# A retention layer and a feed-forward layer on one core: the last turned layer's weight operands get places of their own, and the order tables are written anew

## The chip, the core and the metric

One core of a Trainium2 chip runs the whole kernel. The engines' names are those of the profile: PE (TensorE matmuls) and PEld (its weight loads), DVE (VectorE), ACT (ScalarE), POOL (GpSimd) and SP (SyncE, which here only issues DMAs). SBUF is the core's on-chip memory, PSUM the memory that PE writes. The metric is the device time of one execution in microseconds (us); less is better.

## The reference

```python
gamma = 1.0 - 2.0 ** (-5.0 - np.arange(H)); scale = 1.0 / np.sqrt(D)
for t in range(S):                                  # B, H, S, D = 4, 8, 768, 64
    state = gamma * state + np.einsum('bhd,bhe->bhde', k[:, :, t], v[:, :, t])
    y[:, :, t] = scale * np.einsum('bhd,bhde->bhe', q[:, :, t], state)
x = y.transpose(0, 2, 1, 3).reshape(B * S, H * D)   # 3072 tokens of 512
h = x @ w_in                                        # 512 -> 2048
sp = np.maximum(h, 0.0) + np.log1p(np.exp(-np.abs(h)))
return (h * erf(sp)) @ w_out                        # 2048 -> 512
```

All arrays are float32.

## The kernel before, in words

The retention is computed in chunks of the sequence: within a chunk by masked scores, and across chunks by a carried state. For each chunk q, k and v are loaded, scaled (L795 and L804 on DVE, products of two SBUF tiles; the latter on ACT, L800, in some chunks) and transposed (L813). The results are the rows of x, 256 tokens at a time.

The feed-forward layer takes its first 512 tokens by plain matmuls: `hidden` (L1121) and `project` (L1161). A few of these projections are left over and placed among the later work (`('proj', tile, from, to)` in the tables). The other 2560 tokens use a fast multiplication: 26 products of sums take the place of the plain block products. The sums of the weights (30 of them, `W_SUMS`) are made once, for `w_in` at L614 on DVE or POOL, and for `w_out` at L1477 on POOL or by ACT and an accumulating DMA (L1482, L1487). The `w_out` operands are then stored to a DRAM tile `w_out_d` (`spill`, L1452). The sums of the activations (`X_ORDER`) are made on DVE.

The 2560 tokens are five macros of 512. A macro is four first layers, `first_layer(g)`, and one turned layer, `second_layer(M)`:

- A first layer makes h for a group, 26 products of two matmuls of 128 columns (L1260). Each product's result in PSUM is read into the SBUF tile `arena`: added by DVE (L1274), or, on the first touch of a part, copied by DVE (L1277, L1279; those that `F_DVE` names) or by ACT (L1281, L1283). The very first group is plain (`PLAIN`). After it come softplus and erf on ACT (L1307), and four halves of the gate h·erf, each 1024 columns or two times 512, on DVE or POOL (L1316).
- A turned layer is 26 products of four matmuls of 256 columns (L1391), in the profile eight matmul records each. They hold the `w_out` operand as stationary weights and stream the gated block or a sum of gated blocks. Block sums (L1378, `add`) run on POOL, and in the last macro on DVE. Products are read from four PSUM banks into the result tile `R` (L1399, L1403 and L1405 on DVE, L1401 on ACT). A finished part is transposed by DVE (L1438) and goes out in four DMAs of 32 KB (L1441), by `put`.

The stationary operand of each product is loaded from `w_out_d` into one of four slots of a ring, `WS` (`load_operand`, L1334, 256 KB each). `refill`, ahead of each product, keeps four operands loaded beyond those used. The queue of each load is a letter of `LOAD_FIRST`, `LOAD_LATER` or `LOAD_LAST` (y is SP, s ACT, g POOL); `LOAD_LAST` is 12 times SP and then 14 times ACT.

The order of all this is written out in tables. Every engine and every DMA queue works in the order in which the program issues. For each kind of first layer (0 to 3 in the first macro, a to d in the middle ones, w to z in the last) a row of `AT` has two lists. The first says what is issued behind which of the 26 products: `prod` is one turned product of the macro before, `chunk` one step of the next chunk's preparation, `gate`, `erf`, `op` a sum of w_out, `in` and `in0` sums of w_in, `kick` a wait of POOL for DVE (a DVE copy of one column, L1343, which a POOL copy reads, L1344). The second says what comes behind them all. Further tables give the order of the products (`F_ORDER`; `FIRST_STEPS`, `S_STEPS` and `LAST_STEPS` for the turned layers), which W_in sums are POOL's (`W_IN_POOL`), and what stands ahead of the first first layer (`PRE`).

The turned layer of a macro starts while the first layers of the next one run (`prod`), so that its products fill PE between first-layer products. The last macro has no successor: behind its last first layer come two gates of 1024 columns on DVE, the rest of the turned layer before it, and then all but the first three products of its own turned layer:

```python
    for half in range(2):
        gate(NG - 1, half)
    while active:
        product()
```

`w_in_sb`, the SBUF tile with the 26 operands of W_in, has two halves (`s`) used by first layers in turn; nothing reads a half again behind its last first layer.

Of the kernel before, what the change touches and what calls it, by code (L numbers as in the profile page):

```python
# [23 lines left out]
P = 128  # L24
# [12 lines left out]
N_W, N_X = 26, 18  # L37
# [98 lines left out]
X_ORDER = (1, 0, 2, 6, 5, 12, 13, 9, 4, 7, 14, 8, 15, 3, 17, 10, 16, 11)  # L136
# [4 lines left out]
W_ORDERED = (0, 1, 2, 4, 16, 3, 5, 6, 10, 7, 20, 15, 24, 8, 13, 9, 17, 11, 23, 28, 26, 25, 12, 18, 21, 14, 22, 29, 19, 27)  # L141
# [4 lines left out]
AT = {0: ([(1, 'prod'), (1, 'chunk'), (2, 'spill'), (2, 'spill'), (3, 'in', 19), (6, 'in', 16), (6, 'op'), (8, 'in0', 4),  # L146
      (8, 'in', 3), (8, 'prod'), (9, 'in', 2), (9, 'put', 0), (9, 'prod'), (9, 'in0', 8), (11, 'op'), (12, 'op'),
      (12, 'proj', 1, 0, 2), (12, 'in0', 14), (13, 'in', 25), (13, 'in', 26), (13, 'spill'), (13, 'in', 7),
      (14, 'kick'), (14, 'kick'), (15, 'chunk'), (16, 'chunk'), (16, 'in', 6), (16, 'spill'), (16, 'idle'),
# [5 lines left out]
     [('rest',), ('softplus',), ('proj', 2, 2, 4), ('xs', 3), ('begun',), ('xs', 4), ('prod',), ('prod',),  # L155
      ('proj', 2, 1, 2), ('xs', 1), ('proj', 3, 1, 2), ('in', 30), ('xs', 3), ('prod',), ('prod',), ('xs', 13)]),
 1: ([(1, 'in0', 27), (1, 'proj', 1, 2, 4), (2, 'kick'), (2, 'op'), (3, 'in0', 30), (4, 'prod'), (5, 'kick'), (5, 'op'),
      (5, 'chunk'), (5, 'op'), (7, 'prod'), (8, 'op'), (9, 'chunk'), (10, 'erf', 1), (10, 'gate', 0, 0, 'g'),
      (13, 'prod'), (16, 'chunk'), (17, 'gate', 0, 1, 'v'), (18, 'kick'), (18, 'idle'), (20, 'in', 3), (21, 'put', 2),
      (22, 'chunk'), (24, 'put', 1), (24, 'gate', 1, 0, 'g'), (24, 'gate', 1, 1, 'v'), (26, 'op')],  # L160
     [('rest',), ('xs', 2), ('xs', 4), ('softplus',), ('prod',), ('prod',), ('begun',), ('xs', 15), ('prod',),
      ('proj', 3, 3, 4), ('prod',), ('xs', 1), ('xs', 2)]),
 2: ([(1, 'op'), (1, 'chunk'), (1, 'prod'), (1, 'put', 3), (2, 'kick'), (6, 'op'), (10, 'erf', 1),
      (11, 'gate', 0, 0, 'g'), (11, 'prod'), (13, 'gate', 1, 1, 'g'), (13, 'gate', 1, 0, 'g'), (13, 'gate', 0, 1, 'g'),
      (14, 'op'), (15, 'chunk'), (17, 'op'), (17, 'op'), (18, 'prod'), (20, 'op'), (20, 'chunk'), (20, 'chunk'),
      (21, 'op'), (23, 'refill'), (25, 'op'), (25, 'idle')],
     [('rest',), ('prod',), ('xs', 1), ('xs', 14), ('prod',), ('softplus',), ('xs', 5), ('prod',), ('xs', 2),
      ('begun',), ('prod',), ('xs', 2)]),
# [15 lines left out]
 'c': ([(1, 'chunk'), (1, 'gate', 1, None, 'v'), (5, 'chunk'), (5, 'chunk'), (8, 'next'), (13, 'chunk'), (13, 'prod'),
        (15, 'prod'), (17, 'chunk'), (20, 'gate', 0, 1, 'v'), (21, 'idle'), (24, 'chunk'), (25, 'gate', 0, 0, 'v'),
        (26, 'chunk'), (26, 'kick'), (26, 'prod')],
       [('rest',), ('xs', 3), ('refill',), ('begun',), ('softplus',), ('erf', 0), ('prod',), ('prod',), ('xs', 2),
        ('xs', 5), ('xs', 8), ('prod',), ('prod',), ('xs', 6)]),
 'd': ([(1, 'chunk'), (2, 'kick'), (3, 'chunk'), (6, 'gate', 1, None, 'g'), (7, 'gate', 0, None, 'g'), (10, 'new'),
        (10, 'chunk'), (12, 'chunk'), (14, 'prod'), (17, 'chunk'), (18, 'chunk'), (24, 'chunk'), (26, 'idle')],  # L190
       [('rest',), ('softplus',), ('refill',), ('xs', 7), ('erf', 0), ('begun',), ('prod',), ('append',), ('prod',),
        ('xs', 8), ('prod',), ('xs', 3), ('prod',), ('xs', 1)]),
 'w': ([(1, 'chunk'), (2, 'gate', 1, None, 'v'), (2, 'gate', 0, None, 'v'), (3, 'prod'), (6, 'chunk'), (6, 'kick'),
        (7, 'next'), (10, 'idle'), (12, 'chunk'), (12, 'chunk'), (13, 'prod'), (14, 'chunk'), (19, 'chunk'),
        (22, 'chunk'), (25, 'prod')],
# [4 lines left out]
        (23, 'prod'), (24, 'chunk'), (26, 'chunk')],  # L200
# [3 lines left out]
        (6, 'next'), (8, 'prod'), (11, 'chunk'), (11, 'chunk'), (12, 'chunk'), (13, 'prod'), (16, 'chunk'),  # L204
        (19, 'chunk'), (21, 'idle'), (26, 'prod'), (26, 'chunk')],
       [('rest',), ('softplus',), ('refill',), ('prod',), ('begun',), ('erf', 0), ('xs', 5), ('prod',), ('xs', 6),
        ('xs', 3), ('xs', 8), ('prod',), ('prod',), ('xs', 2)]),
 'z': ([(1, 'chunk'), (1, 'gate', 0, None, 'g'), (3, 'gate', 1, 1, 'v'), (4, 'kick'), (4, 'prod'),
        (5, 'gate', 1, 0, 'v'), (5, 'chunk'), (6, 'kick'), (7, 'chunk'), (10, 'idle'), (14, 'chunk'), (15, 'kick'),
        (15, 'kick'), (15, 'chunk'), (20, 'new'), (20, 'chunk'), (26, 'chunk')],  # L210
       [('rest',), ('refill',), ('softplus',), ('xs', 5), ('erf', 0), ('prod',), ('prod',), ('begun',), ('xs', 4),
# [35 lines left out]
BEGUN = {0: 'smMb',  # L247
 1: 'smMb',
 2: 'smMb',
 3: 'smMb',  # L250
 'a': 'smbM',
 'b': 'smbM',
 'c': 'sMmb',
 'd': 'sMmb',
 'w': 'smbM',
 'x': 'smbM',
 'y': 'sMbm',
# [1536 lines left out]
```

## Time and profile before

| | |
|---|---|
| median of 3 runs | 668.21 us (664.67 to 668.76) |
| profiled execution, its own time | 662.88 us |
| its span (first to last instruction) | 660.8 us |
| mean granted PE clock | 0.996 |
| PE busy | 645.8 us, 6112 matmuls |
| DVE, ACT, POOL busy | 483.8, 309.9, 298.0 us |
| block sums on POOL (L1378) | 75 of 2361 ns |
| turned matmuls (L1391) | 1040, 235.9 us busy |
| operand loads (L1334) on ACT, on SP | 102, 20 |

The profile is of one execution. Its own time is lower than the three timed runs, which are of the same program; sums of durations from it belong to 662.88. "Busy" counts the time in which an engine executes, so 98% for PE means that 15 us of the span are left without a matmul. A granted clock under 1 means that matmuls ran slower in a part of the time; that time counts as busy. The stages that are told apart below: first the plain part and the sums, to 155 us; the first macro's first layers, to 210; the repeated part of first layers with turned products between them, to 593; the last first layer's end, to 607.4; the last turned layer, to 656.2; the last outputs.

### The profile page before, as it was taken

Reading aid. Unit: us, or ns where it says so; the run is one execution under the profiler, and the core shown is the slowest. Engines: PE = TensorE matmul, PEld = TensorE weight load, DVE = VectorE, ACT = ScalarE, POOL = GpSimd, SP = SyncE. Lnnn points to the kernel's source line nnn. Section 1 sums busy time; section 2 is a strip of 40 time slices with the busy share of each in tenths; the row PEclk is TensorE's granted clock in tenths of the full one; section 3 lists DMA queues with packets and bytes.
Section 4 is the critical chain, followed back from the end, with each engine's and each line's share of the span. In section 5 each row is a group of like instructions: output and inputs, shape, how many; then the busy total and the mean of one; then the engine's idle time right before and its main releaser. Section 6 shows DMA issues by size and latency. Waiting matters only on the chain.

```text
span 660.8 us, 16104 instructions
## 1 busy us (share of the span) xinstructions
PE 645.8 (98%) x6112; PEld 544.0 (82%) x6112; DVE 483.8 (73%) x1148; ACT 309.9 (47%) x527; POOL 298.0 (45%) x251
## 2 busy tenths in 40 slices
PE   8999999998899999999999999999999999999897
PEld 7744444476798999999989999999999999999786
DVE  5999889995888846767856857856856944856683
ACT  3468594433574654455453455463554542533200
POOL 1000063767457687316565337475237368344000
PEclk9999999999999999999999999999999999999999
DMA  9999886776557455464564564554554521342565
GB/s 188 231 261 237 173 245 110 135 192 142 146 135 211 109 135 124 106 144 97 132 137 95 139 135 100 134 139 94 128 123 105 127 81 48 110 95 58 155 172 116
DMA packets 221597, 91.55 MB, mean 139 GB/s; under 512 B 185808, under 2 KB 200272, under 8 KB 221520
## 3 DMA queue, kind: packets, MB, share of 16 engines
q1 hardware_dynamic: 198720, 51.50, 38.0%
q10 hardware_dynamic: 17888, 27.08, 14.4%
q0 software_dynamic: 4912, 11.94, 6.6%
q8 instruction: 48, 0.79, 0.5%
q14 instruction: 29, 0.24, 0.1%
HBM read 74.47 MB, written 13.11 MB: 133 GB/s over the span
## 4 chain that ended last, share of the span: by engine, by line
PE 91%; DVE 3%; DMA 2%; SPq 1%; issue 1%; ACT 0%; POOL 0%; DVEq 0%; ACTq 0%; POOLq 0%
PE o L1391 33%; PE hp L1260 18%; PE r L1260 14%; PE hp L1121 8%; PE o L1161 7%; PE r L1037 1%; PE hp L893 1%; PE r L1047 1%; PE hp L990 1%; DVE arena L1274 1%; SPq L373 1%; PE r L1235 1%; DMA kq<-in_k_dram 1%; PE o L750 1%; PE r L779 1%
## 5 line engine op out<-in xcount | busy, mean ns | idle before, releaser
L1391 PE MATMUL o<-arena 128*128 128x256 f32 x1040 | 235.9, 381 | 1.7 <-DMA arena<-w_out_d 1.7
L1391 PEld LDWEIGHTS o<-arena 128*128 128x128 f32 x1040 | 193.0, 190 | 27.1 <-DVE arena L1399 2.1
L1378 POOL TENSOR_TENSOR arena<-arena 128x1024 f32<-128x1024 f32 x75 | 175.8, 2361 | 20.0 <-PE o L1391 15.7
L1260 PE MATMUL hp<-xs,w_in_sb 128*128 128x128 f32 x812 | 118.8, 278 | 2.1 <-DVE arena L1274 2.0
L1260 PEld LDWEIGHTS hp<-xs,w_in_sb 128*128 128x128 f32 x812 | 106.0, 193 | 4.8 <-DVE arena L1274 2.1
L1274 DVE TENSOR_TENSOR arena<-arena,hp 128x256 f32<-128x256 f32 x184 | 75.1, 417 | 25.6 <-PE hp L1260 17.2
L1260 PE MATMUL r<-xs,w_in_sb 128*128 128x128 f32 x632 | 92.4, 277 | 0.5 <-ACT arena L1281 0.2
L1344 POOL COPY idle_out<-turn 128x1 f32<-128x1 f32 x45 | 13.0, 289 | 157.4 <-DVE turn L1343 157.4
L1260 PEld LDWEIGHTS r<-xs,w_in_sb 128*128 128x128 f32 x632 | 81.9, 193 | 2.2 <-issue 0.8
L1399 DVE TENSOR_TENSOR arena<-arena,o 128x256 f32<-128x256 f32 x90 | 37.1, 417 | 63.4 <-PE o L1391 61.4
L1274 DVE TENSOR_TENSOR arena<-arena,r 128x256 f32<-128x256 f32 x158 | 62.8, 416 | 17.6 <-PE r L1260 13.6
L1121 PE MATMUL hp<-xT,w_in_sb 128*128 128x512 f32 (+2 forms) x144 | 56.5, 548 | 0.0
L1260 PE MATMUL hp<-xT,w_in_sb 128*128 128x128 f32 x296 | 45.7, 277 | 3.5 <-DVE arena L1279 1.8
L1121 PEld LDWEIGHTS hp<-xT,w_in_sb 128*128 128x128 f32 x144 | 25.8, 190 | 27.0 <-issue 24.6
L1260 PEld LDWEIGHTS hp<-xT,w_in_sb 128*128 128x128 f32 x296 | 39.8, 192 | 5.7 <-issue 2.6
L1281 ACT COPY arena<-r 128x256 f32<-128x256 f32 x53 | 19.7, 373 | 51.6 <-PE r L1260 21.4
L1056 ACT COPY xT<-r 128x256 f32<-128x256 f32 x33 | 10.8, 375 | 63.0 <-PE r L1047 63.0
L1316 POOL TENSOR_TENSOR arena<-arena,e_even 128x1024 f32<-128x1024 f32 (+1 forms) x19 | 36.3, 1926 | 8.5 <-ACT e_even L1307 8.5
L1307 ACT ACTIVATE e_even<-e_even 128x2048 f32<-128x2048 f32 x20 | 38.2, 1912 | 0.2
L1401 ACT ACTIVATE arena<-o 128x256 f32<-128x256 f32 x25 | 9.3, 378 | 58.8 <-PE o L1391 58.8
L1260 PE MATMUL r<-xT,w_in_sb 128*128 128x128 f32 x236 | 36.2, 276 | 0.3 <-DVE arena L1274 0.2
L722 POOL COPY idle_out<-arena 128x1 f32<-128x1 f32 x1 | 0.6, 592 | 78.9 <-ACT arena L1139 78.9
(185 smaller groups left out, 972.5 us busy)
## 6 DMA issues: line engine op xcount, KB each, us to landing
arena<-w_out_d ACTq DMA_DIRECT2D x102, 256.0 KB, 2.8
arena<-in_moe_w_out_dram SPq DMA_DIRECT2D x12, 512.0 KB, 6.1
kq<-in_k_dram SPq DMA_DIRECT2D x23, 256.0 KB, 4.3
v<-in_v_dram SPq DMA_DIRECT2D x23, 256.0 KB, 3.4
arena<-w_out_d SPq DMA_DIRECT2D x20, 256.0 KB, 3.0
out_dram<-arena SPq DMA_DIRECT2D x154, 32.0 KB, 2.5
kq<-in_q_dram SPq DMA_DIRECT2D x284, 16.0 KB, 2.3
kb<-in_k_dram SPq DMA_DIRECT2D x276, 16.0 KB, 2.4
```

The lines of the kernel that those rows point to most:

```text
L1056: nc.scalar.copy(x[r], pp[r][:, :2, :])
L1121: nc.tensor.matmul(HP_[ft][:, t], w_in_of(ft, kk), XC[0][:, kk, t], start=(kk == 0), stop=(kk == n_k - 1),)
L1161: nc.tensor.matmul(O[0][tt].rearrange("p (c x) -> p c x", c=4), E[g][:, u * TCH + tt * P : u * TCH + (tt + 1) * P], w_out_of(ft), start=(f ...
L1260: nc.tensor.matmul(to[:, u, :], w_in_sb[:, s, w, u * P : (u + 1) * P], x_at(x), start=first and u == 0, stop=True, skip_group_check=True,)
L1274: nc.vector.tensor_tensor(h, h, of, op=ALU.add if plus else ALU.subtract)
L1281: nc.scalar.copy(h, of)
L1307: nc.scalar.activation(e_even[:, at], e_even[:, at], AF.Erf)
L1316: engine.tensor_tensor(x, x, e_even[:, half * BL : (half + 1) * BL][:, at], op=ALU.mult)
L1344: nc.gpsimd.tensor_copy(idle_out, turn)
L1378: engine.tensor_tensor(block(blocks[to]), *ins, op=OP[sign])
L1391: nc.tensor.matmul(to, WS[:, used % 4, u], rhs[:, u * 2 * P : (u + 1) * 2 * P], start=first and u == 0, stop=True, skip_group_check=True,)
L1399: nc.vector.tensor_tensor(r, r, to, op=ALU.add if plus else ALU.subtract)
```

## The change

The last turned layer's 26 operands no longer pass through the ring. `tail_operand(k)` is a place in `w_in_sb`: operands 0 to 12 lie in the half that the next-to-last first layer read, 13 to 25 in that of the last one. `load_tail` issues one load on the queue that `TAIL` names, SP for all. Thirteen are issued behind odd products of the last first layer, and then one behind each product of the last turned layer. `refill` and `load_operand` stop ahead of them, and `LOAD_LAST` is gone.

```diff
     def load_operand():
-        if loaded < len(W_ORDER):
+        if loaded < len(W_ORDER) - N_W:
...
+    def tail_operand(k):
+
+        s, at = (NG - 2 - G0 + k // 13) % 2, k % 13 * 2
+        return w_in_sb[:, s, at : at + 2].rearrange("p a (u c) -> p (a u) c", c=P)
+
+    def load_tail():
+
+        nonlocal tail_loaded
+        k = tail_loaded
+        ENGINES[TAIL[k]].dma_start(
+            tail_operand(k).rearrange("p u c -> p (u c)"), w_out_d[W_ORDER[len(W_ORDER) - N_W + k]]
+        )
+        tail_loaded += 1
...
         def multiply(n, at):
+            in_tail = used - (len(W_ORDER) - N_W)
+            operand = WS[:, used % 4] if in_tail < 0 else tail_operand(in_tail)
             for u in range(FG):
                 nc.tensor.matmul(
-                    to, WS[:, used % 4, u], rhs[:, u * 2 * P : (u + 1) * 2 * P],
+                    to, operand[:, u], rhs[:, u * 2 * P : (u + 1) * 2 * P],
...
             used += 1
+            if in_tail >= 0 and tail_loaded < N_W:
+                load_tail()
...
     def refill():
-        while loaded < min(used + 4, len(W_ORDER)):
+        while loaded < min(used + 4, len(W_ORDER) - N_W):
...
             for at, *what in during:
                 if at == n:
                     act(*what)
+            if g == NG - 1:
+                for _ in range(TAIL_AT.count(n)):
+                    load_tail()
...
-LOAD_LAST = 'yyyyyyyyyyyyssssssssssssss'
+TAIL = 'yyyyyyyyyyyyyyyyyyyyyyyyyy'
+TAIL_AT = (1, 3, 5, 7, 9, 11, 13, 15, 17, 19, 21, 23, 25)
```

The order tables are written anew at the same time. The last turned layer's order, cut to its first part (the items `('sum', ...)` are block sums, the numbers are products):

```diff
-LAST_STEPS = (('sum', 5, ...), ('sum', 0, ...), 'F', ('sum', 1, ...), 3, 0,
- ('sum', 6, ...), 21, ('sum', 9, ...), 1, ('sum', 12, ...), ('sum', 7, ...),
- 11, 5, ('sum', 8, ...), 20, 7, ('sum', 4, ...), 9, 4, ('sum', 13, ...), 13,
+LAST_STEPS = (('sum', 5, ...), 'F', ('sum', 0, ...), ('sum', 1, ...), 3,
+ ('sum', 6, ...), 21, ('sum', 9, ...), 1, 0, ('sum', 12, ...),
+ ('sum', 7, ...), 11, 5, ('sum', 8, ...), 20, ('sum', 4, ...), 9, 4,
+ ('sum', 13, ...), 7, 13,
```

In `AT`, items move by a few products in every kind. The first lists of the second and the fourth first layer of the first macro, as examples:

```diff
- 1: ([(1, 'in0', 27), (1, 'proj', 1, 2, 4), (2, 'kick'), (2, 'op'), (3, 'in0', 30), (4, 'prod'), (5, 'kick'), (5, 'op'),
-      (5, 'chunk'), (5, 'op'), (7, 'prod'), (8, 'op'), (9, 'chunk'), (10, 'erf', 1), (10, 'gate', 0, 0, 'g'),
-      (13, 'prod'), (16, 'chunk'), (17, 'gate', 0, 1, 'v'), (18, 'kick'), (18, 'idle'), (20, 'in', 3), (21, 'put', 2),
-      (22, 'chunk'), (24, 'put', 1), (24, 'gate', 1, 0, 'g'), (24, 'gate', 1, 1, 'v'), (26, 'op')],
+ 1: ([(1, 'in0', 27), (2, 'kick'), (2, 'in0', 30), (2, 'op'), (4, 'in', 9), (4, 'prod'), (4, 'op'),
+      (5, 'proj', 1, 2, 3), (5, 'kick'), (5, 'op'), (5, 'chunk'), (7, 'prod'), (8, 'op'), (9, 'in', 24), (9, 'chunk'),
+      (13, 'prod'), (14, 'erf', 1), (16, 'chunk'), (17, 'gate', 0, 1, 'v'), (18, 'kick'), (18, 'idle'),
+      (20, 'proj', 3, 0, 1), (20, 'gate', 0, 0, 'g'), (20, 'in', 3), (21, 'put', 2), (22, 'chunk'), (24, 'put', 1),
+      (24, 'gate', 1, 0, 'g'), (24, 'gate', 1, 1, 'v'), (26, 'op')],
...
- 3: ([(1, 'chunk'), (4, 'kick'), (5, 'chunk'), (11, 'erf', 1), (14, 'gate', 1, 0, 'v'), (17, 'gate', 0, 1, 'v'),
-      (18, 'prod'), (19, 'idle'), (19, 'free'), (23, 'gate', 1, 1, 'v'), (23, 'chunk'), (23, 'gate', 0, 0, 'v'),
-      (24, 'new'), (26, 'chunk')],
+ 3: ([(1, 'chunk'), (5, 'chunk'), (10, 'erf', 1), (14, 'gate', 1, 0, 'v'), (16, 'prod'), (19, 'chunk'), (19, 'idle'),
+      (20, 'gate', 0, 1, 'v'), (20, 'free'), (23, 'gate', 1, 1, 'v'), (23, 'gate', 0, 0, 'v'), (24, 'new'),
+      (26, 'chunk')],
```

In kind c one gate of 1024 columns becomes two of 512. `F_DVE` gets one more part in kinds 3 and x (DVE instead of ACT makes the first read). `BEGUN`, the order of four steps at the start of a chunk, becomes the same in all kinds. One load of `LOAD_FIRST` goes from ACT's queue to POOL's. `PRE`, `EARLY`, `X_ORDER`, `W_ORDERED`, `F_ORDER` of kind 0, `W_IN_ORDER`, `W_IN_POOL` (12 entries, before 14), `FIRST_STEPS`, and the load order of one chunk are changed in the same manner. The number of matmuls, their shapes, the block sums, the products and the output DMAs stay.

More of the change, by code (lines that the diff above doesn't have):

```diff
@@ new lines @@
+AT = {0: ([(1, 'prod'), (1, 'chunk'), (2, 'spill'), (2, 'spill'), (3, 'in', 19), (4, 'proj', 0, 0, 1), (6, 'in', 16),
[4 rows of a table added]
+      (17, 'spill'), (18, 'in', 8), (18, 'proj', 3, 2, 3), (18, 'op'), (20, 'in0', 18), (20, 'spill'), (20, 'idle'),
+      (21, 'spill'), (21, 'in', 10), (21, 'op'), (22, 'in0', 22), (22, 'spill'), (22, 'kick'), (22, 'kick'),
+      (22, 'spill'), (22, 'op'), (22, 'op'), (22, 'spill'), (22, 'chunk'), (23, 'in', 5), (25, 'in', 8), (25, 'op'),
+      (26, 'in', 16), (26, 'op'), (26, 'kick'), (26, 'spill'), (26, 'in0', 24)],
+     [('rest',), ('softplus',), ('proj', 2, 2, 4), ('begun',), ('xs', 3), ('xs', 3), ('prod',), ('prod',), ('xs', 5),
+      ('xs', 2), ('in', 30), ('prod',), ('prod',), ('xs', 11)]),
+ 1: ([(1, 'in0', 27), (2, 'kick'), (2, 'in0', 30), (2, 'op'), (4, 'in', 9), (4, 'prod'), (4, 'op'),
[3 more added lines that the diff above has]
+      (24, 'gate', 1, 0, 'g'), (24, 'gate', 1, 1, 'v'), (26, 'op')],
+     [('rest',), ('xs', 4), ('xs', 2), ('softplus',), ('prod',), ('prod',), ('begun',), ('xs', 15), ('prod',),
+      ('proj', 3, 3, 4), ('prod',), ('xs', 2), ('xs', 1)]),
+ 2: ([(1, 'put', 3), (1, 'op'), (1, 'kick'), (4, 'chunk'), (5, 'prod'), (6, 'op'), (10, 'kick'), (10, 'erf', 1),
+      (11, 'gate', 0, 0, 'g'), (12, 'kick'), (13, 'gate', 1, 1, 'g'), (13, 'gate', 1, 0, 'g'), (13, 'prod'),
+      (13, 'gate', 0, 1, 'g'), (15, 'chunk'), (15, 'op'), (17, 'op'), (17, 'op'), (18, 'prod'), (20, 'op'),
+      (20, 'chunk'), (20, 'chunk'), (21, 'op'), (23, 'refill'), (25, 'op'), (25, 'idle'), (26, 'kick')],
+     [('rest',), ('prod',), ('xs', 2), ('prod',), ('softplus',), ('xs', 14), ('xs', 5), ('prod',), ('xs', 1), ('prod',),
+      ('begun',), ('xs', 2)]),
+ 3: ([(1, 'chunk'), (5, 'chunk'), (10, 'erf', 1), (14, 'gate', 1, 0, 'v'), (16, 'prod'), (19, 'chunk'), (19, 'idle'),
+      (20, 'gate', 0, 1, 'v'), (20, 'free'), (23, 'gate', 1, 1, 'v'), (23, 'gate', 0, 0, 'v'), (24, 'new'),
+      (26, 'chunk')],
+     [('rest',), ('begun',), ('prod',), ('append',), ('xs', 8), ('prod',), ('xs', 2), ('prod',), ('softplus',),
+      ('xs', 5), ('erf', 0), ('xs', 4), ('prod',)]),
+ 'a': ([(1, 'chunk'), (3, 'gate', 1, None, 'v'), (5, 'prod'), (5, 'gate', 0, None, 'v'), (6, 'next'), (9, 'chunk'),
+        (14, 'prod'), (16, 'chunk'), (19, 'chunk'), (22, 'chunk'), (24, 'chunk'), (25, 'idle'), (26, 'chunk'),
@@ L180 @@
         (7, 'prod'), (14, 'prod'), (16, 'chunk'), (18, 'kick'), (18, 'chunk'), (22, 'prod'), (22, 'chunk'),
-        (26, 'kick'), (26, 'idle'), (26, 'chunk')],
+        (25, 'kick'), (26, 'idle'), (26, 'chunk')],
        [('rest',), ('refill',), ('xs', 1), ('softplus',), ('erf', 0), ('begun',), ('prod',), ('xs', 5), ('prod',),
         ('xs', 2), ('xs', 7), ('prod',), ('xs', 9), ('prod',)]),
- 'c': ([(1, 'chunk'), (1, 'gate', 1, None, 'v'), (5, 'chunk'), (5, 'chunk'), (8, 'next'), (13, 'chunk'), (13, 'prod'),
-        (15, 'prod'), (17, 'chunk'), (20, 'gate', 0, 1, 'v'), (21, 'idle'), (24, 'chunk'), (25, 'gate', 0, 0, 'v'),
-        (26, 'chunk'), (26, 'kick'), (26, 'prod')],
+ 'c': ([(1, 'chunk'), (1, 'gate', 1, 0, 'v'), (1, 'gate', 1, 1, 'v'), (5, 'chunk'), (5, 'chunk'), (8, 'next'),
+        (13, 'chunk'), (13, 'prod'), (15, 'prod'), (17, 'chunk'), (20, 'gate', 0, 1, 'v'), (23, 'idle'), (24, 'chunk'),
+        (25, 'gate', 0, 0, 'v'), (26, 'chunk'), (26, 'kick'), (26, 'prod')],
@@ L187 @@
        [('rest',), ('xs', 3), ('refill',), ('begun',), ('softplus',), ('erf', 0), ('prod',), ('prod',), ('xs', 2),
[L188 to L192, printed above, removed]
@@ L193 @@
- 'w': ([(1, 'chunk'), (2, 'gate', 1, None, 'v'), (2, 'gate', 0, None, 'v'), (3, 'prod'), (6, 'chunk'), (6, 'kick'),
-        (7, 'next'), (10, 'idle'), (12, 'chunk'), (12, 'chunk'), (13, 'prod'), (14, 'chunk'), (19, 'chunk'),
-        (22, 'chunk'), (25, 'prod')],
+        ('xs', 5), ('xs', 8), ('prod',), ('xs', 6), ('prod',)]),
+ 'd': ([(1, 'chunk'), (2, 'kick'), (3, 'chunk'), (6, 'gate', 1, None, 'g'), (6, 'chunk'), (7, 'gate', 0, None, 'g'),
+        (10, 'new'), (12, 'chunk'), (14, 'prod'), (17, 'chunk'), (19, 'chunk'), (24, 'chunk'), (26, 'idle')],
+       [('rest',), ('softplus',), ('refill',), ('xs', 6), ('erf', 0), ('begun',), ('xs', 9), ('prod',), ('append',),
+        ('prod',), ('xs', 3), ('prod',), ('prod',), ('xs', 1)]),
@@ L196 @@
+ 'w': ([(1, 'chunk'), (2, 'gate', 0, None, 'v'), (2, 'gate', 1, None, 'v'), (3, 'prod'), (6, 'chunk'), (7, 'next'),
+        (10, 'idle'), (12, 'chunk'), (13, 'prod'), (14, 'chunk'), (15, 'chunk'), (19, 'chunk'), (22, 'chunk'),
+        (23, 'kick'), (25, 'prod')],
        [('rest',), ('refill',), ('begun',), ('softplus',), ('prod',), ('erf', 0), ('prod',), ('xs', 4), ('prod',),
@@ L203 @@
  'y': ([(1, 'gate', 1, 0, 'v'), (2, 'gate', 0, 0, 'v'), (3, 'gate', 1, 1, 'v'), (4, 'gate', 0, 1, 'v'), (5, 'chunk'),
-        (6, 'next'), (8, 'prod'), (11, 'chunk'), (11, 'chunk'), (12, 'chunk'), (13, 'prod'), (16, 'chunk'),
+        (6, 'next'), (8, 'prod'), (10, 'chunk'), (11, 'chunk'), (12, 'chunk'), (13, 'prod'), (14, 'chunk'),
         (19, 'chunk'), (21, 'idle'), (26, 'prod'), (26, 'chunk')],
        [('rest',), ('softplus',), ('refill',), ('prod',), ('begun',), ('erf', 0), ('xs', 5), ('prod',), ('xs', 6),
[L207 to L211, printed above, removed]
+        ('xs', 3), ('xs', 2), ('xs', 8), ('prod',), ('prod',)]),
+ 'z': ([(1, 'chunk'), (1, 'gate', 0, None, 'g'), (3, 'gate', 1, 1, 'v'), (4, 'kick'), (4, 'prod'), (5, 'chunk'),
+        (5, 'gate', 1, 0, 'v'), (5, 'chunk'), (6, 'kick'), (10, 'idle'), (14, 'chunk'), (15, 'kick'), (15, 'kick'),
+        (15, 'chunk'), (17, 'new'), (20, 'chunk'), (26, 'chunk')],
+       [('rest',), ('refill',), ('softplus',), ('xs', 4), ('erf', 0), ('prod',), ('prod',), ('begun',), ('xs', 5),
         ('append',), ('xs', 4), ('prod',), ('xs', 6), ('prod',)])}
@@ L246 @@
  'z': 'hrhr'}
[L247 to L257, printed above, removed]
- 'z': 'smbM'}
-F_ORDER = {0: (0, 2, 6, 3, 1, 4, 5, 7, 8, 9, 10, 11, 12, 13, 14, 16, 15, 17, 18, 20, 19, 21, 22, 23, 24, 25),
+BEGUN = {0: 'msMb',
+ 1: 'msMb',
+ 2: 'msMb',
+ 3: 'msMb',
+ 'a': 'msMb',
+ 'b': 'msMb',
+ 'c': 'msMb',
+ 'd': 'msMb',
+ 'w': 'msMb',
+ 'x': 'msMb',
+ 'y': 'msMb',
+ 'z': 'msMb'}
+F_ORDER = {0: (0, 2, 6, 3, 1, 4, 5, 7, 9, 8, 10, 11, 13, 12, 14, 16, 15, 17, 18, 19, 21, 22, 23, 20, 24, 25),
  1: (3, 0, 2, 4, 6, 1, 7, 10, 5, 8, 9, 11, 12, 13, 16, 14, 15, 20, 17, 18, 21, 22, 19, 23, 24, 25),
@@ L279 @@
  'w': (2, 3),
- 'x': (2, 5),
+ 'x': (0, 2, 5),
  'y': (0, 1, 2, 4),
@@ L1388, in multiply @@
             to = banks[bank][:, : 2 * P]
+            in_tail = used - (len(W_ORDER) - N_W)
+            operand = WS[:, used % 4] if in_tail < 0 else tail_operand(in_tail)
+            assert in_tail < tail_loaded, "tail"
             rhs = block(blocks[x])
```

72 lines of the change are left out of this document (30 added, 42 removed), and 25 rows, old and new, of tables (AT, FIRST_STEPS, LAST_STEPS).

## The prediction

> **What bounds the kernel now.** I read the page first: each engine's busy share, then the share of each engine in the chain that ended last.
>
> ```profile
> PE 645.8 (98%) x6112; PEld 544.0 (82%) x6112; DVE 483.8 (73%) x1148; ACT 309.9 (47%) x527; POOL 298.0 (45%) x251
> PE 91%; DVE 3%; DMA 2%; SPq 1%; issue 1%; ACT 0%; POOL 0%; DVEq 0%; ACTq 0%; POOLq 0%
> ```
>
> TensorE (PE) works 645.8 of 660.8 us and the change leaves its 6112 matmuls as they are. So nothing can be gained but idle PE time (15.0 us) and time at a lower clock. Next, the busy times by stage, to see where that idle time lies (core and bounds, length; then the busy time of PE, PEld, DVE, ACT, POOL; the granted PE clock, the DMA share, GB/s).
>
> ```profile
> 127.00:155.00 28.00, 28.00 (x266) 19.56 (x265) 23.82 (x52) 8.17 (x18) 18.21 (x23) 1.00 0.63 150
> 155.00:210.00 55.00, 49.06 (x575) 43.13 (x574) 45.17 (x111) 29.43 (x49) 32.15 (x36) 0.97 0.63 169
> 210.00:593.00 383.00, 382.77 (x4156) 357.69 (x4155) 259.19 (x720) 183.99 (x351) 208.99 (x122) 1.00 0.50 115
> 593.00:607.40 14.40, 14.01 (x114) 13.48 (x113) 9.76 (x29) 3.74 (x8) 5.82 (x9) 1.00 0.25 67
> 607.40:656.20 48.80, 47.09 (x219) 40.83 (x217) 32.10 (x49) 6.80 (x8) 2.15 (x1) 1.00 0.55 146
> ```
>
> The long repeated part, 210 to 593, is PE from end to end (0.23 us idle). Two stages have idle PE: the first macro's first layers, 155 to 210 (5.94), and the last turned layer, 607.4 to 656.2 (1.71). I read the timeline of both. The first, around its longest stop (start, length, engine, line, operation):
>
> ```profile
> 160.47 3.10 DVE L795 TENSOR_TENSOR kq<-kq,q_b 128x512 f32<-128x512 f32 x1
> 160.64 1.03 POOL L614 TENSOR_TENSOR w_in_sb<-w_in_sb 128x256 f32<-128x256 f32 x1
> 161.45 1.55 POOL L1477 TENSOR_TENSOR arena<-arena 128x512 f32<-128x512 f32 x1
> 161.51 0.61 PE L1260 MATMUL r<-xs,w_in_sb 128*128 128x128 f32 x4
> 163.49 0.41 DVE L1279 TENSOR_SCALAR arena<-hp 128x256 f32<-128x256 f32 x1
> 163.95 0.94 PE L1260 MATMUL hp<-xT,w_in_sb 128*128 128x128 f32 x4 [1.83 <-DVE arena L1279]
> 164.69 2.01 PE L1260 MATMUL hp<-xs,w_in_sb 128*128 128x128 f32 x8
> ...
> 165.34 2.25 DVE L804 TENSOR_TENSOR v<-v,kq_s 128x512 f32<-128x512 f32 x1
> 165.73 1.30 POOL L1477 TENSOR_TENSOR arena<-arena 128x512 f32<-128x512 f32 x1
> ```
>
> L795, a DVE product of two SBUF tiles that usually takes 0.68, takes 3.10 where two POOL sums of SBUF tiles lie beside it. The PSUM read L1279 is queued behind it, PE waits 1.83 for that, and then PE's clock falls: eight matmuls of 128 columns take 2.01 at 164.69 where eight elsewhere take 0.89. The granted clock is 0.73 in 165 to 170. Then L804 (2.25; 0.69 when alone) beside another POOL sum costs PE two waits of 0.51. The second, at the start of the last turned layer:
>
> ```profile
> 607.47 7.07 PE L1391 MATMUL o<-arena 128*128 128x256 f32 x32
> 608.47 4.69 SPq L1441 DMA_DIRECT2D out_dram<-arena  x8
> ...
> 613.27 1.81 SPq L1334 DMA_DIRECT2D arena<-w_out_d  x4
> 613.35 2.36 DVE L1316 TENSOR_TENSOR arena<-arena,e_even 128x1024 f32<-128x1024 f32 x2 [1.94 <-ACT e_even L1307]
> 615.63 0.41 DVE L1399 TENSOR_TENSOR arena<-arena,o 128x256 f32<-128x256 f32 x1
> ...
> 616.24 1.10 PE L1391 MATMUL o<-arena 128*128 128x256 f32 x4 [1.70 <-DMA arena<-w_out_d]
> ```
>
> PE runs four products (32 matmul records, 8 a product) and then stands 1.70: the next operand's load sits on SP's queue behind eight output DMAs, goes out at 613.27 and lands 2.84 later. After that 23 products follow in 39.97 us, 1.74 each, with no gap.
>
> **The change, part by part.**
>
> 1. *The tail's operands.* Before, 12 loads on SP and 14 on ACT go into a ring of four slots. After, 26 loads go out on SP, 13 of them at every second product of the last first layer, into memory that no later matmul reads. A load takes 0.3 to 0.4 to issue on SP and lands 2.4 to 4.9 after, so the fifth operand is there 10 us early: −1.7. Late next is DVE: the gates end at 615.71 and the reads of the products before are queued behind them. The order of the last products is new: 1 and 0 come fourth and fifth where 0, 21, 1 stood, and 4, 7 change places. In it the sixth product, by my count, starts at 616.2 in a bank whose earlier read is ACT's (L1401, 613.22 plus 0.64), and the eighth needs DVE's read of the sixth, done near 619.45 against a start of 619.6. With the old order two waits of some 0.8 would have stood there. I take −1.7, bounds −1.9 to −0.1. SP issues 26 loads of 0.35 = 9.1 and some 38 output DMAs of 0.59 (4.69 / 8) = 22.4 in 65 us; ACT loses 14 issues. Of the second 13 loads, one goes out behind each product, 13 products ahead of use: 22 us for a landing of 2.4 to 4.9. So the output DMAs that wait for DVE's transposes on the same queue are covered; without that cover each late load costs up to what it cost here, 1.7.
>
> 2. *The stop at 160 to 164.* The tables move one of the two plain projections of the first stage from ahead of product 2 to behind 5, and the other to 20, send two sums of W_in (L614) to other places, and add waits of POOL for DVE (L1343, L1344). Following the new order with the old durations, DVE and POOL come to L795 at nearly the same time as before, with one POOL sum beside it rather than two. The stop before was 1.83 for 3.10 − 0.68 = 2.4 of stretch; with one sum of 1.27 beside it the stretch is some 1.3 and I take −0.9 for the stop (bounds 0 to −1.8, and +0.3 if a third sum joins).
>
> 3. *The clock.* At the lower clock PE lost about 1.6: 1.1 on the eight matmuls, 0.4 on four at 166.49 (1.06 for 0.61, ends included), 0.1 to 0.3 on those at 163.95. Stops of 1.3 at 180.63 and 1.70 at 616.24 were followed by no such slow matmuls. So a stop of 0.9 would mostly not bring it: six times in ten, −1.0; bounds 0 and −1.6. [...]
>
> 4. *L804 at 165.34.* It moves with L795; POOL's sum beside it is one place further: half of two waits of 0.51, −0.5 (bounds 0, −1.0).
>
> 5. *A gate of the fourth first layer* (half of 1024 columns, L1316) ran 1.57 beside POOL at 204 where others take 0.65 to 0.69. It moves from product 17 to 20, past that sum: 0.9 of DVE, of which PE felt about half: −0.5 (bounds 0, −0.9).
>
> 6. *Everything else*: chunk steps one or two products earlier or later, some gates as two halves (16 of 1024 and 18 of 512 become 13 and 24; a half costs 0.65 for 1.18 / 2, so 0.07 each, 0.4 in all), two more reads on DVE for ACT (0.42 each), two W_in sums from POOL to DVE (0.61 each), four instructions for the two added waits (0.15 and 0.19 to 0.48). They lie in stages where PE is busy 382.77 of 383.00, 28.00 of 28.00: DVE has 259 of 383 there and room. Cost 0. Without that cover it is 0.4 + 0.8 + 1.2 + 1.0 = 3.4 at most if nothing hid any of it; a new stop is priced below. The stop of 1.31 at 180.63 (PE waits for a load of q) I leave, 0 (bounds ±1.3): its queue, SP, has the same loads ahead.
>
> Sum: −1.7 − 0.9 − 1.0 − 0.5 − 0.5 = −4.6. The profiled execution took 662.88 (span 660.8 and 2.1 around it), so 658.3. The median of the runs shown is 668.21 (664.67 to 668.76): the profiled execution lies 5.3 below it, and I carry the difference over: 668.21 − 4.6 = **663.6**.
>
> **Rivals.**
>
> *Only the tail.* The meeting of L795 with POOL is not resolved, it only moves: −1.7 − 0.5 = −2.2, 666.0. For: in my count L795 still starts within 1 us of a POOL sum. Against: one sum fewer.
>
> *L795 runs free.* Then −1.7 − 1.8 − 1.6 − 1.0 − 0.9 = −7.0, 661.2. For: 0.5 us of shift suffices. L795 started 0.17 ahead of L614 and yet took 3.10, so who starts first did not save it here. [...]
>
> *The tail's wait stays*: the loads sit behind output DMAs on SP after all, or DVE's reads take over: the 1.7 is kept, only −2.9 × 0.5 of the rest holds: −1.4, 666.8. Against: two loads, four output DMAs and eleven loads stand in SP's queue before the layer begins.
>
> *Slower: a new meeting in the repeated part.* L795 and L804 come one or two products earlier there, up to 0.9 us; POOL runs block sums of 2.36 each (175.8 of its 298 us). If L795 falls beside one, the stretch is up to 2.4, the PSUM read behind it is late, PE stops 2.0 and loses 1.6 by the clock: 3.6, in the same place in each of four macros, 14.4 − 4.6 = +9.8, 678.0. It decides from two such places on (7.2 against 4.6). For: same order in each macro, and 0.23 us of idle says that the old places were free of it. Against: the new places fall, with old durations, into gaps of POOL of 2 to 3 us.
>
> **How the numbers follow.** My forecast 0.42, own range 660.5 to 666.5; only the tail 0.20; L795 free 0.19; tail's wait stays 0.06; slower 0.13. A measurement of this kernel (three runs within 0.6%, the profiled one 0.8% below the median) tells about 1% from no change: 661.5 and 674.9. Below 661.5 lie two thirds of "free" (0.13), a third of the forecast (0.14) and 0.04 of the others: 0.31. Above 674.9: 0.12. Range: below, the sum of the far ends (−1.9 − 1.8 − 1.6 − 1.0 − 0.9 = −7.2, 661.0) and 4 for runs near the profiled one; above, 666.8 and 3 for one new stop: 657 to 670, with most of the slower case outside.
>
> **What would show it.** Right: PE idle under 0.3 between the fifth and sixth products of the last turned layer; no wait on w_out_d loads; L795 of the first macro's second stage under 2.2; granted clock 1.00 in 165 to 170; PE busy in 155 to 210 up to some 51 of a stage 3 shorter; idle in the repeated part below 0.5. Wrong: an idle group of L1260 waiting for L1274 in the repeated part, an L795 mean above 1 us, or a clock below 0.97 anywhere after 210.

## The result, and the profile after

| | before | after |
|---|---|---|
| median, first comparison | 666.44 us (663.31 to 668.76, 4 runs) | 656.84 us (656.05 to 657.34, 4 runs) |
| profiled execution (span) | 662.88 (660.8) | 656.86 (655.0) |
| ratio, first comparison | | 0.9858, 95% interval 0.9809 to 0.9907 |
| ratio, run again with 23 and 6 runs | | 0.9912, 0.9890 to 0.9934 |

The change makes the kernel faster, by 9.6 us in the first comparison and by 5.8 (a ratio of 0.9912 of 663 us) when both were run again. The forecast was 663.6 with a range down to 657.0: the time lies just below it. The profiled executions alone differ by 6.0, where my sum had 4.6. One execution of the kernel before took 1344.18 us and is in none of the figures here and below.

The page of the changed kernel:

```profile
PE 643.3 (98%) x6112; PEld 542.3 (83%) x6112; DVE 483.6 (74%) x1157; ACT 309.2 (47%) x525; POOL 299.6 (46%) x252
PE 93%; DMA 2%; DVE 2%; SPq 2%; issue 1%; ACT 1%; POOL 0%; DVEq 0%; ACTq 0%; POOLq 0%
```

The same 6112 matmuls take 2.5 us less PE time: none was removed, so this is clock for the most part (mean granted clock 0.996 before and 1.000 after; the prediction put the loss behind the one slow stretch at 1.6). Its stages, with the columns of the table of before:

```profile
155.00:210.00 55.00, 50.99 (x714) 45.20 (x712) 46.27 (x124) 31.30 (x53) 37.19 (x42) 1.00 0.66 175
210.00:593.00 383.00, 382.19 (x4044) 357.39 (x4041) 258.73 (x722) 183.49 (x351) 208.06 (x123) 1.00 0.50 115
593.00:607.40 14.40, 14.01 (x107) 13.27 (x106) 10.98 (x30) 5.08 (x6) 7.63 (x7) 1.00 0.69 213
```

The granted clock in 155 to 210 is 1.00 and was 0.97. Idle PE there fell from 5.94 to 4.01. The repeated part lost a little: 0.81 idle in place of 0.23. The loads moved into 593 to 607 show as a DMA share of 0.69, which was 0.25, and cost PE nothing. The place of the longest stop, in the timeline of the changed kernel (L622 was L614, L803 was L795, L812 was L804, L1505 was L1477, L1515 was L1487):

```profile
159.06 0.78 POOL L622 TENSOR_TENSOR w_in_sb<-w_in_sb 128x256 f32<-128x256 f32 x1
...
159.56 0.83 DVE L803 TENSOR_TENSOR kq<-kq,q_b 128x512 f32<-128x512 f32 x1
...
159.79 0.92 POOL L1515 DMA_DIRECT2D arena<-arena  x1
...
160.44 1.57 POOL L1505 TENSOR_TENSOR arena<-arena 128x512 f32<-128x512 f32 x1
...
162.09 1.27 POOL L1505 TENSOR_TENSOR arena<-arena 128x512 f32<-128x512 f32 x1
162.15 1.75 DVE L812 TENSOR_TENSOR v<-v,kq_s 128x512 f32<-128x512 f32 x1
...
164.38 0.80 PE L1268 MATMUL hp<-xs,w_in_sb 128*128 128x128 f32 x5 [0.94 <-DVE arena L1282]
```

L803 starts 0.23 before POOL's DMA issue (L1515) and meets only the last 0.28 of the POOL sum ahead of that issue (L622, to 159.84): it takes 0.83, not 3.10. L812 still meets a sum, and PE stops 0.94 behind it. The tail, at the start of the last turned layer (L1417 was L1391):

```profile
603.82 1.89 PE L1417 MATMUL o<-arena 128*128 128x256 f32 x8
...
604.83 5.38 SPq L1469 DMA_DIRECT2D out_dram<-arena  x8
605.55 19.80 PE L1417 MATMUL o<-arena,w_in_sb 128*128 128x256 f32 x91
...
609.70 2.36 DVE L1324 TENSOR_TENSOR arena<-arena,e_even 128x1024 f32<-128x1024 f32 x2 [0.68 <-ACT e_even L1315]
610.32 5.14 SPq L1359 DMA_DIRECT2D w_in_sb<-w_out_d  x11
```

From 605.55 on the products run without a gap. SP still issues eight output DMAs first and loads behind them, but nobody waits for those loads. One wait, early in the repeated part, was not in the profile of before:

```profile
233.75 3.43 SPq L381 DMA_DIRECT2D kb<-in_k_dram  x5
236.83 3.23 ACTq L1342 DMA_DIRECT2D arena<-w_out_d  x2
237.30 0.91 SPq L1342 DMA_DIRECT2D arena<-w_out_d  x2
...
240.48 1.75 PE L1417 MATMUL o<-arena 128*128 128x256 f32 x7 [0.81 <-DMA arena<-w_out_d]
```

A ring load on SP stands behind small loads of k and goes out at 237.30. PE comes here 4.0 us earlier than in the profile of before (the first-layer matmuls ahead of the product start at 237.72 and started at 241.71), the SP load 2.7 earlier (237.30 for 240.04), and PE waits 0.81 for it.

### The profile page after: what moved, and what is told of

Read it like the earlier page. It is cut to its first block, busy times and chain, and to the rows that moved or that the text cites. A ratio compares the mean times of both kernels' runs of the same rounds, so it can differ in the third digit from the quotient of the medians.

```text
span 655.0 us, 16090 instructions
## 1 busy us (share of the span) xinstructions
PE 643.3 (98%) x6112; PEld 542.3 (83%) x6112; DVE 483.6 (74%) x1157; ACT 309.2 (47%) x525; POOL 299.6 (46%) x252
## 4 chain that ended last, share of the span: by engine, by line
PE 93%; DMA 2%; DVE 2%; SPq 2%; issue 1%; ACT 1%; POOL 0%; DVEq 0%; ACTq 0%; POOLq 0%
PE o L1417 33%; PE hp L1268 18%; PE r L1268 14%; PE hp L1129 8%; PE o L1169 8%; SPq L381 2%; PE r L1045 1%; PE hp L901 1%; PE r L1055 1%; PE hp L998 1%; PE r L1243 1%; PE hp L1243 1%; DVE arena L1282 1%; DMA kq<-in_q_dram 1%; DMA kb<-in_k_dram 1%
## 5 line engine op out<-in xcount | busy, mean ns | idle before, releaser
L1417 PE MATMUL o<-arena 128*128 128x256 f32 x832 | 190.8, 381 | 0.8 <-DMA arena<-w_out_d 0.8
L1417 PEld LDWEIGHTS o<-arena 128*128 128x128 f32 x832 | 153.6, 190 | 20.5 <-DVE kq L803 1.0
L1367 POOL COPY idle_out<-turn 128x1 f32<-128x1 f32 x47 | 14.5, 309 | 155.3 <-DVE turn L1366 155.3
L1417 PE MATMUL o<-arena,w_in_sb 128*128 128x256 f32 x208 | 45.1, 379 | 0.0
L1417 PEld LDWEIGHTS o<-arena,w_in_sb 128*128 128x128 f32 x208 | 39.4, 190 | 5.5
```

Of the source, the lines that this page charges most:

```text
L1367: nc.gpsimd.tensor_copy(idle_out, turn)
L1417: nc.tensor.matmul(to, operand[:, u], rhs[:, u * 2 * P : (u + 1) * 2 * P], start=first and u == 0, stop=True, skip_group_check=True,)
```

## The experiments

All ratios are against the kernel before on the same chip, with 95% intervals; 1% is 6.6 us. The name in code type is the run's label.

**What one execution of the kernel before does not show** (`before_again`). No edit.

> The kernel before, unchanged, to see what one execution of it does not show. The five timed executions so far lie between 662.9 and 668.8 us, those of the changed kernel between 656.1 and 657.3. Theory A (clock): a stop of PE of 1.3 to 2 us is followed in some executions by 3.4 us at half clock, at a cost of 1.6 us each. The kernel before has three such stops (1.99 at 161.8, 1.47 at 178.7, 1.86 at 614.2), the profiled one showed slow matmuls behind one of them only. Then executions differ in steps of some 1.6 us, up to 3 more than the profiled one, and a second trace shows slow matmuls behind another set of these stops and the granted clock of a run falls with its time. Theory B (waits): the executions differ in the length of waits on loads, at granted clocks that are alike. Theory C (chip): on one chip all executions agree within 0.3%, and the spread came from different chips.

Ratio 0.9989 (0.9964 to 1.0015). Theories A and B both hold in part, C falls: on one chip the executions spread over 661 to 668. Over 76 executions of the kernel before, in three comparisons, median 663.6, time falls with the run's mean granted clock (correlation -0.78): median 661.6 in 22 executions at 0.998 or more, 664.0 in 37 at 0.995 to 0.997, 666.0 in 17 below. In the two traces the clock was halved for 3.413 us, once each between the first 10 us and the last matmul, and behind the same stop, the one at 162. The second trace has waits that the first did not have. One is for the ring load near 240, 0.73 at 245.21, so the kernel before can have this wait too. The other:

```profile
119.74 2.48 DVE L1213 TENSOR_TENSOR xs<-xT,xs 128x128 f32<-128x128 f32 x2
119.80 0.89 POOL L1487 DMA_DIRECT2D arena<-arena  x1
120.42 1.58 POOL L1477 TENSOR_TENSOR arena<-arena 128x512 f32<-128x512 f32 x1
122.15 2.42 DVE L1213 TENSOR_TENSOR xs<-xs,xT 128x128 f32<-128x128 f32 x1
...
131.02 1.55 PE L1161 MATMUL o<-arena 128*128 128x512 f32 x3 [0.82 <-DVE arena L1110]
```

DVE's sums of 128 columns (L1213) take 0.28 in the median of the trace of before. Here two take 2.48 together from 119.74 on and the next one 2.42, beside POOL, and PE waits 0.23 and 0.82 at 129 and 131 for the DVE sum queued behind them (L1110).

**The tail alone** (`tail_only`). The diff of the tail shown above on the old tables, `LAST_STEPS` included.

> The kernel before with the tail's operands in W_in's memory and the loads on SP as in the change, all order tables as before, LAST_STEPS too. My sum: the 1.70 wait for the load is gone, but the old order of the last products meets DVE's reads behind the gates, two waits of some 0.8: -0.1 to -1.0 us, with idle PE in front of the sixth and the eighth product of the last turned layer. Theory A adds: no stop of 1.9 there any more, so the median falls by up to 1.6 more (-1.5 to -3). Theory B: -0.1 to -1.9 and as much spread as before.

Ratio 0.9954 (0.9936 to 0.9972), -3.1 us, more than my sum and at the far end of theory A. The wait for the load is gone. Of the two waits of 0.8 that I expected one is there, and half as long: at 621.29 PE has waited 0.33 for DVE's read (L1420), 0.50 between matmul starts.

Three of its six executions have a clock of 0.997 or less, as the stop at 162 stays.

**The tail with the new order of the last products** (`tail_steps`). The order, cut:

```diff
 (tail_only)
-LAST_STEPS = (... 3, 0, ... 21, ... 1, ...
+LAST_STEPS = (... 3, ... 21, ... 1, 0, ...
```

> tail_only with the new order of the last products. My prediction has two waits of some 0.8 in the old order and none in the new; the trace of tail_only shows one of 0.50 at 620.6. So -0.5 against tail_only, -3.6 against the kernel before, and no wait of over 0.1 between 608 and 655. Rival: the reads of DVE are late in the new order at another product: a wait of 0.3 or more.

Ratio 0.9962 (0.9934 to 0.9990). The trace has no wait of PE in the last turned layer, as expected; the 0.5 that this is worth against tail_only can't be seen in the medians.

**The tail by another queue** (`tail_pool`). The ring stays.

```diff
-LOAD_LAST = 'yyyyyyyyyyyyssssssssssssss'
+LOAD_LAST = 'yyygggggggggssssssssssssss'
```

> The kernel before, ring and tables unchanged, but nine of the tail's loads go out on POOL's queue, idle there, in place of SP's, where they sit behind output DMAs. If the queue alone made the wait of 1.7 to 2.1 at the start of the last turned layer, places of their own are not needed: that wait falls below 0.5 and the median by 1.3 to 3, as in tail_only (-3.1). Rival: with a ring of four slots the slot comes free too late whatever the queue (product one ends near 609.2, 5.2 before the load is needed, and POOL works 2.4 on a sum until 609.6): a wait of 0.3 to 1.5 stays, -0.3 to -1.5.

Ratio 0.9960 (0.9930 to 0.9991), the same as tail_only within the intervals.

```profile
605.44 12.36 PE L1391 MATMUL o<-arena 128*128 128x256 f32 x56
606.45 4.88 SPq L1441 DMA_DIRECT2D out_dram<-arena  x8
607.64 0.55 POOL L1334 DMA_DIRECT2D arena<-w_out_d  x1
609.36 0.54 POOL L1334 DMA_DIRECT2D arena<-w_out_d  x1 [1.17 <-PE o L1391]
...
618.13 4.15 PE L1391 MATMUL o<-arena 128*128 128x256 f32 x18 [0.33 <-DVE arena L1399]
```

POOL issues each load when PE frees its slot, and seven products follow without a gap: a ring of four is enough here. What made the wait was SP's queue, so the places in W_in's memory are one remedy of two.

**The tables alone, and their two halves.** First (`tables_only`) the changed kernel with the ring's loads put back in `load_operand`, `multiply` and `refill`:

> The changed kernel with the tail's operands loaded through the ring of four slots as before (LOAD_LAST back), all order tables new. My sum: what the tables bring is -2.9 and the tail's wait of 1.7 to 1.9 stays: 1.7 to 1.9 above the changed kernel. Theory A: 1.9 to 3.5 above the changed kernel in the median, with a spread of 1.6 between executions that comes from that one stop, and -6 to -8 against the kernel before. Theory B: 1.9 above the changed kernel, no more spread than it has.

Ratio 0.9933 (0.9915 to 0.9950), -4.5; PE waits 1.38 for the tail's load again, and yet all six executions have a clock of 0.999 or more: this stop cost its length and no clock. Then (`first_tables`) the kernel before with the first macro's tables only:

> The kernel before with the new tables of the first macro alone (PRE, EARLY, FIRST_STEPS, the rows 0 to 3 of AT, BEGUN, F_ORDER and F_DVE, the orders of the weight sums and the first ring loads); the rows a to z, LAST_STEPS and the ring loads of the tail as before. My sum: -2.9, all of what the tables bring. If the rows a to z bring nothing, this equals tables_only within 0.5 us but for the order of the last products. Theory A: -6 to -7 against the kernel before in the median, since the stop at 161.8 and its clock loss go; B: -2.9 to -4.

Ratio 0.9944 (0.9921 to 0.9966), -3.7, the same within the intervals. Theory A's -6 was too much. Its trace has a longer wait (2.33) for the ring load near 240, and one of 2.35 for the tail's load. This edit also holds two things that the text above it does not name: the queues of one more chunk's loads, and the chunk's load order that the next run has too. Then (`rest_tables`) the rest of the tables:

> The kernel before with the new tables of the repeated part alone: rows a to z of AT, their BEGUN, F_DVE of kind x, LAST_STEPS and one chunk's load order; the first macro and the ring loads as before. My sum: 0 (PE was busy 382.77 of 383.00 there), -0.2 to +0.5. Rival: the rows a to z carry a part of the gain, -1 to -2; tables_only and first_tables, 0.2 apart, speak against it.

Ratio 0.9999 (0.9975 to 1.0024): no gain can be seen from the rows of the repeated part, as forecast, though the interval (-1.7 to +1.6 us) does not rule out the smaller end of the rival. This trace shows the half clock behind both stops, the one at 162 and the one of the tail:

```profile
165.00:170.00 5.00, 4.35 (x22) 3.89 (x22) 3.37 (x8) 3.27 (x3) 4.46 (x5) 0.66 0.46 161
...
615.00:620.00 5.00, 3.93 (x10) 3.19 (x11) 0.94 (x3) 0.00 (x0) 0.00 (x0) 0.66 0.56 194
620.00:625.00 5.00, 5.00 (x25) 4.39 (x24) 4.49 (x7) 0.42 (x2) 0.00 (x0) 1.00 0.55 138
```

The clock is 0.66 in 165 to 170 and again in 615 to 620, where a matmul record takes 0.39 (3.93 / 10) and in the next 5 us 0.20 (5.00 / 25). So the tail's wait can cost clock on top of itself.

**One meeting taken away** (`no_meeting`). In the kernel before, two sums of w_out and POOL's wait for DVE ahead of them are moved in one row.

```diff
- ... (4, 'prod'), (5, 'kick'), (5, 'op'), (5, 'chunk'), (5, 'op'), (7, 'prod'), ...
+ ... (4, 'prod'), (5, 'chunk'), (7, 'kick'), (7, 'op'), (7, 'op'), (7, 'prod'), ...
```

> The kernel before with one thing moved: in row 1 of AT the two sums of w_out (L1477 on POOL, with their wait for DVE) come behind product 7 and not around L795 at product 5; everything else as before. Theory of the meeting (a DVE instruction with two SBUF inputs stands still as long as POOL's instructions follow each other): L795 there falls from 3.1 to at most 1.7 (the sum of W_in, L614, is still near), the stop of 1.99 in front of the first matmul behind it to at most 0.6, and with it the 3.4 us at half clock that two traces show just behind it. Profile -2 to -3.6 us, median -2 to -3.5, few executions at a clock of 0.991 to 0.997. Rival (the stop only moves: POOL's sums now meet L804 and the reads behind it): a stop of over 1 us between 163 and 172, -1 to +0.5 in the median.

Ratio 0.9960 (0.9943 to 0.9978), -2.7.

```profile
159.90 0.92 POOL L1487 DMA_DIRECT2D arena<-arena  x1 [2.67 <-ACT arena L1281]
160.34 1.80 DVE L795 TENSOR_TENSOR kq<-kq,q_b 128x512 f32<-128x512 f32 x1
160.55 1.03 POOL L614 TENSOR_TENSOR w_in_sb<-w_in_sb 128x256 f32<-128x256 f32 x1
...
162.53 0.71 PE L1260 MATMUL hp<-xT,w_in_sb 128*128 128x128 f32 x4 [0.50 <-DVE turn L1343]
```

L795 takes 1.80, a little over the 1.7 that I allowed, and PE's wait falls from 1.83 to 0.50. All 12 executions have a clock of 0.998 or more. The rival's new stop does not come (0.68 before 170.31 is the longest nearby).

**Tail and meeting together** (`built_up`), on otherwise old tables: tail_steps with the edit of no_meeting.

> The kernel before with three things only: the tail's operands in W_in's memory, the new order of the last products, and the two sums of w_out moved behind product 7 in row 1 of AT (as in no_meeting). Every other table as before. If the change's gain is the tail and one meeting of DVE with POOL: the gains add, -1.8 by the tail's wait and -2.6 as no_meeting, and the clock losses behind both go, -5 to -6.5 us, within 1 us of the changed kernel; executions at clocks of 0.998 to 1.000. If the other new tables carry a part: -3 to -4.5.

Ratio 0.9906 (0.9876 to 0.9936), -6.2, against 0.9912 for the whole change run again (`after_again`):

> The changed kernel, unchanged, against the kernel before on one chip. The medians of tail_only (-3.3) and tables_only (-4.5) add up to -7.8. If the two parts do not touch each other and the first three times of the kernel before (median 668.2) were a high draw: -7 to -8 us, 0.988 to 0.990, and executions within 1.5 us of each other at clocks of 0.998 to 1.000. If a further gain comes only with both parts together (the 9.6 of the first comparison): 0.985 to 0.986.

The gain at hand is -5.8 (-7.3 to -4.4), short of the -7 to -8 that I expected; only the end of the interval reaches them. The six executions lie 2.8 apart, not 1.5. So two causes, the tail's wait and the one meeting, are enough for the gain within these intervals. Why it is less than tail_only and tables_only added up (-7.5 by their ratios) stays open. The 9.6 of the first comparison is not repeated; the kernel before had a median of 666.4 in those four executions and 663.6 in the 76 others.

**Two further steps on the changed kernel** (`after_load2`, `after_best`). The wait at 240, by one letter:

```diff
-LOAD_FIRST = 'yygygygssyysssssgggyysssss'
+LOAD_FIRST = 'yygygygsssysssssgggyysssss'
```

> The changed kernel with one letter of LOAD_FIRST changed: the tenth operand of the first turned layer is loaded by ACT's queue instead of SP's. In the changed kernel PE waits 0.8 at 239.4 for a load that SP issues behind 16 small loads of k. If the queue is the cause: that wait is gone, -0.8 us. Rival: the load is late on any queue, since its slot comes free late, or the eleventh operand, still on SP, is late in its place: -0.2 to +0.5.

Ratio 0.9891 (0.9872 to 0.9911), median 655.58, beside 0.9912 and 657.28 for the changed kernel on the same chip: lower by some 0.2%, with intervals that overlap. In its trace the wait is gone: the product starts at 240.09 and has waited for nothing. And L812's meeting:

```diff
- ... (5, 'kick'), (5, 'op'), (5, 'chunk'), (7, 'prod'), (8, 'op'), (9, 'in', 24), (9, 'chunk'), ...
+ ... (5, 'chunk'), (7, 'prod'), (9, 'in', 24), (9, 'chunk'), (10, 'kick'), (10, 'op'), (10, 'op'), ...
```

> after_load2 (the changed kernel with the tenth operand's load on ACT's queue) with the sums of w_out at products 5 and 8 of row 1 of AT moved behind product 10, since L812 there still takes 1.75 beside a POOL sum and PE stops 0.95 to 1.1 behind it. Theory of the meeting: L812 takes 0.7 to 0.9, that stop falls to 0.3 or less: -0.7 to -1.0 below after_load2, 6.5 to 8 below the kernel before. Rival: the moved sums meet a gate or leave the operands' stores late: the same or up to +1.

Ratio 0.9874 (0.9845 to 0.9903), median 656.02. L812 takes 0.68, as expected, and the matmuls behind it at 163.69 wait for nothing; a wait of 0.61 stays at 165.63, and a new one of 0.66 stands at 224.74. Both beat the kernel before by more than their intervals; that either beats the changed kernel, or this one the other, is likely and not shown.

## Why the prediction was wrong, point by point

*The base.* I carried the difference between one profiled execution and a median of three over to the sum. The median, 668.2, was a high draw: 76 later executions have 663.6. Why it was high stays open. This step, with its "4 for runs near the profiled one", put both ends of the range too high; from 663.6 the same sum gives 659.0, and its far ends (-7.2) 656.4, which holds 656.84. So of the 6.8 between forecast and measured time 4.6 are the base, and 2.2 the terms of the sum, above all 2 and 3 below.

*1, the tail.* Right in place and size: 1.70 gone. That the old order would lose it again was overdone: one wait of 0.33 to 0.5, not two of 0.8. Not seen: POOL's idle queue would have done the same.

*2, the stop at L795.* The failed term of the sum. I counted -0.9, with DVE and POOL arriving as before and a whole POOL sum beside L795; measured, the stop of 1.99 (by matmul starts, beyond their usual spacing) fell to 0.30. DVE came 0.23 ahead of POOL's DMA issue, where it had come 0.48 behind it, and met only the last 0.28 of one sum. The rival "L795 runs free", with 0.19, was right here. My reason against it, that L795 had started 0.17 ahead of L614, left out a row: POOL's DMA issue L1487 was under way since 159.99. In both traces with this order of arrival L795 ends a little less than its undisturbed 0.68 after the end of POOL's run, as if it had only started there: 163.57 against 163.00 before, 162.14 against 161.58 in no_meeting. Before, L795 lasted through L614, L1344 and L1477, which followed each other. A DMA issue that came with DVE's product under way did not hold it up: in the changed kernel L803 ends at 160.39, 0.55 after L622, while the issue L1515 runs and just ahead of POOL's next sum (160.44). So L795 was long (3.10, and 1.80 in no_meeting) where the DMA issue stood at the start of POOL's run, and L803 short (0.83) where it came inside it; no run tries this by itself, and why it is so stays open.

*3, the clock.* I took six tenths of one loss of 1.6. The median execution of before has one such loss, and 17 of 76 about two or more (the groups above lie 2.4 and 2.0 apart); the changed kernel has none in 9 of 10. What goes with it is the stop at 162, and no_meeting takes both away by one move: of 114 executions of kernels that have it (before, tail_only, tail_steps, tail_pool, rest_tables) 78 ran at a clock of 0.997 or less, of 54 without it 2. So most of the loss was gained.

*4 and 5, L804 and the gate.* Counted at -0.5 each; nothing was gained. L812 takes 1.75 and the longest PE wait behind it is 0.94, not 0.51. The gate takes 1.76 at 200.24 where it took 1.57: beside it lay two DMA issues of POOL (from 199.98 on) and its next sum (from 201.32 on).

*6, everything else at 0.* Right for the rows a to z as far as 0.9999 can tell. Two misses. One is the wait of 0.81 near 240, against my signs (no wait for a `w_out_d` load, idle PE under 0.5 in the repeated part). With this load on SP it is 0.62 to 2.33 in the four traces with the new first-macro tables; with the old tables it is 0 in five traces, 0.21 and 0.27 in two, and 0.73 in before_again. The other is the meeting at 119 to 126. It cost nothing in the profiled execution, and PE was idle for 0.43 to 1.28 of 100 to 155 in three of the other seven traces with the old first-macro tables (before_again, tail_only, rest_tables). With the new ones that was 0 in four traces and 0.24 and 0.34 in two. A stage that is fully busy in one trace is not proof that its cover holds in all. Whether the W_in sums moved from POOL to DVE make this difference was not tried.

By the traces: the tail -1.8, L795's stop -1.7, the clock -1.6, the wait near 240 +0.8, L804's place +0.3 (stops of 0.82 and 0.68 became 1.10 and 0.68): -4.0 of the 5.8 between the spans. The remaining -1.8 I did not trace to single places. As a whole, PE's idle time fell by 3.3 (15.0 to 11.7) and its busy time by 2.5.

## What to carry to other kernels

Before summing against one profile, compare several executions: if their granted clocks differ, a stop of 2 us cost its length here and, in part of the executions, some 1.6 more in clock. A transfer that stood behind others on one queue was helped by an idle queue as well as by new memory (0.9960 in tail_pool, 0.9954 in tail_only); try the letter first. When a hand-made order moves an engine earlier by a few us, look which queue does not move with it.

## What was not expected of the hardware

Between the first 10 us and the last matmul the halved clock came in pieces of 3.413 us, four in the fourteen traces. In the trace of before, the full-clock pieces ahead of the half one and behind it are 157.013 and 491.519 us, 46 and 144 times 3.4133. Counted in such pieces, the one just ahead of each of these four had PE idle for 1.83 to 1.97 of its 3.41 us (1.83 in before, from 160.87 to 164.28). Behind pieces with as much idle time the clock was full in three cases (tail_only and tail_steps at the stop at 162, first_tables near 240 with 1.95); the four are before, before_again and twice rest_tables. In before it was full (1.00) behind the pieces with the next most idle time, 1.40 (614.84 to 618.26, the tail's wait) and 1.31 (177.94 to 181.35). So the idle time in the piece alone does not decide; what does stays open.
